# Streaming attention pairs of batch 0 with joint scores, and a new order of the kernel's head

## The chip, the cores and the metric

The kernel runs on one core of a Trainium2 chip. The metric is the device time of one launch in microseconds (us); lower is better. The kernel before took 227.66 us in the median of three runs (226.22 to 230.84).

## What is computed

The input is an attention layer (4 batches, 8 heads, 768 positions, 64 channels a head) and a two-layer MLP. Three heads (0, 2 and 6) are retrieval heads with a full causal mask. The other five are streaming heads: a position sees the 4 first positions and the 64 latest ones.

```python
scores = (1 / sqrt(64)) * q @ k.T
mask   = causal                       if retrieval head
         causal & (sink | in_window)  otherwise          # sink: key < 4, window: 64
a      = softmax(where(mask, scores, -1e9))
x      = (a @ v)                      # heads side by side: [3072, 512]
h      = x @ w_in                     # [512, 2048]
g      = maximum(h, 0) + alpha * minimum(h, 0)
out    = g @ w_out                    # [2048, 512]
```

## The kernel before

**Units of work.** A segment n is a pair of heads of one batch: batch n // 4, heads PAIRS[n % 4] of (2, 6), (1, 5), (0, 4), (3, 7). So in each batch pair 0 is two retrieval heads, pairs 1 and 3 are two streaming heads, and pair 2 has one of each. Batch 0 (n below 4) is handled in a way of its own: its masks are added on PE as extra matmuls (the identity times a mask of -30000) rather than multiplied in afterwards on DVE.

**Steps of a segment,** with the letters that the order uses:

- Lq, Lk, Lv: loads of q, k and v as fp32. SP issues them, but for the first half of k of pair 0 (`load_k`, L230), which ACT issues. Lq0 is split by head into Lq0.0 and Lq0.1.
- Cq, Ck, Cv: casts to bf16. The strings CQ, CK and CV (L303 to L305) say for each n which engine does it: V is DVE, A is ACT, P is POOL. A cast of v in batch 0 is followed by a small copy of the sink rows for each streaming head (`sinks`, L308), on POOL by default.
- Tq, Tk: transposes on PE (`to_array`); tq, tk: the copies of them out of PSUM (`put_q`, `put_k`). For streaming heads `put_k` lays the keys out in 7 slots of 128 (sinks and window) with three copies (L400 to L402). Each head has a key array of its own, of 128 rows, of which its own 64 hold keys and the others zeros (items kz0 to kz3 clear them).
- S, s: scores on PE (`S_retr`, `S_stream`) and their exponentials on ACT (`E_retr`, `E_stream`). A streaming head of batch 0 has 7 score matmuls, over all 128 rows, and 7 mask matmuls, in thirds of 384 columns; its exponentials are one of two thirds and one of one.
- A, a: attention times v on PE (`AV`), and the division by the sum on DVE.
- X, x: transposes of the result into xT (on PE and DVE in batch 0, by DMA later).
- P, p, g: the first projection (`P1`), the negative part on ACT (`relu`) and the combination on DVE (`prelu`). P0.f.part is the projection of the first 512 positions for one block f of 128 of the 2048 columns; for f below 6 it is cut into the parts that need pairs 0 and 1, pair 2, and pair 3. t = 0 and t = 1 are batch 0.
- O, o: the second projection and its way out. L, l: the last piece of it.
- wi0 to wi7 and wo0 to wo3: loads of w_in and w_out, issued by POOL. wi0 and wi1 hold the two halves of the contraction for f 0 to 3, wi2 and wi3 for f 4 to 7, wi4 and wi5 for 8 to 11, wi6 and wi7 for 12 to 15.
- warm0 to warm8: groups of matmuls on a zero tile (L698), which compute nothing.
- id, nms, nmr, zero, one, vz, qz, sz, so, kfz, nz: constants and clears.

**Order.** ORDER (L14) is a list of all these items, written by a planner, and `kernel` issues them in that order (L817). An engine runs its own instructions in the order in which they were issued; waits across engines follow from the data. A DMA that POOL issues stands in POOL's own queue between its casts and clears. SP has the loads alone in the head.

**PSUM.** Eight banks. Scores of batch 0 take a pair of banks out of (0, 1) and (2, 3).

The head of ORDER, up to the projections P1.8, P0.8 and P0.10, covers the loads, casts and attention of batch 0 and the first blocks of its projection. In this head POOL's queue has, as far as the prediction needs it: Ck3.1, Ck3.0, wi1, wi0, Cq3, Cv1 and its two sink copies, two clears, Cv2 and its sink copy, a clear, wi6, wi7, wi5, wi4, Cv3.0.

Of the kernel before, what the change touches and what calls it, by code (L numbers as in the profile page):

```python
# [14 lines left out]
vz2 id busy warm4 warm0 warm5 vz0 qz0 Lq0.0 sz2 so2 Lq0.1 zero vz3 nms Lk1 Lq1 sz1  # L15
Cq0.1 nmr Ck1.1 kz1 La Lk0 Ck1.0 kz0 Cq1 Cq0.0 Tq0.0 Ck0.0 Tk0.0 tk0.0 Lk2 Ck2.0 Lv0 warm2
tq0.0 S0.0.0 s0.0.0 qz S0.0.1 Tk1 warm3 warm6 vo kz2 Ck0.1 vz1 Ck2.1 Tq1 s0.0.1 tq1 Tq0.1 tk1.1
S0.0.2 s0.0.2 Cv0 tk1.0 m4.0.2 warm7 tq0.1 Lq2 S1.1.0 Tk0.1 tk0.1 S1.0.0 ro0 s1.1.0 Tk2 tk2.1 idf Cq2
s1.0.0 S0.1.0 s0.1.0 A0.0 S0.1.1 s0.1.1 S0.1.2 Tq2 warm8 s0.1.2 tq2 S1.1.1 s1.1.1 A0.1 kz3 sz0 Lk3 Ck3.1
Lv1 S1.0.1 m4.1.2 a0.0 s1.0.1 Al Ck3.0 Lq3 tk2.0 Tk3 S2.0.1 s2.0.1 a0.1 tk3.1 al X0 x0 S2.0.2  # L20
Lv2 Lv3 so1 so0 Lq5 wi1 s2.0.2 Lk4 m8.0.2 wi0 Cq3 Tq3 S2.0.0 s2.0.0 tk3.0 Cv1 tq3 A1.0
a1.0 Lk5 kfz2 A1.1 a1.1 kfz0 S2.1.0 S2.1.1 Cv2 s2.1.1 kfz3 wi6 A2.0 a2.0 wi7 S3.1.0 s2.1.0 s3.1.0
wi5 wi4 S3.0.0 A2.1 Cv3.0 s3.0.0 X1 S3.1.1 s3.1.1 S3.0.1 a2.1 X2 x1 x2 m8.1.2 near2 Ck4.0 P0.0.0
wi2 s3.0.1 A3.0 Cv3.1 P0.3.0 a3.0 P0.2.0 P0.2.1 A3.1 Ck4.1 Lk7 Lk6 P0.1.0 P0.1.1 P0.0.1 Tk4 tk4.0 Cq5
m14.0.2 a3.1 X3 nz1 tk4.1 x3 Tq5 P0.3.1 tq5 P1.2 p1.2 P1.0 p1.0 g1.0 P0.1.2 wi3 P0.13 Lq4
one p0.1 g0.1 P0.2.2 Lq6 Lv7 p0.2 P0.0.2 P1.14 p1.14 g1.2 g1.14 Ck5.0 Ck5.1 nr Tk5 tk5.1 P0.3.2
tk5.0 g0.2 p0.0 g0.0 p0.3 g0.3 P0.12 p0.12 g0.12 p0.13 g0.13 P0.14 nz0 kfz1 P1.8 P0.8 wo0 p0.8
g0.8 P0.10 S5.1.1 s5.1.1 P0.15 p0.15 wo1 wo2 wo3 ns p1.8 g0.15 g1.8 P0.11 p0.11 p0.14 g0.14 p0.10
S5.0.0 Lv5 P0.7 g0.10 P0.6 Ck6.1 P0.4.0 Lq7 P0.4.1 Lk8 Ck6.0 s5.0.0 p0.7 S5.0.2 s5.0.2 Cq4 Tq4 tq4
g0.11 P0.4.2 P0.9 Ck7.1 Ck7.0 S5.1.0 p0.9 g0.9 P1.4 s5.1.0 p1.4 Lv6 S4.0.1 Cq6 m12.1.2 P0.5.0 s4.0.1 P0.5.1  # L30
P0.5.2 P1.12 m5.0.0 g1.4 S4.0.3 g0.7 p0.4 p0.5 m5.1.0 g0.4 g0.5 Cv5 P1.10 S5.0.1 p1.10 s5.0.1 near0 p0.6
g0.6 O0.1.0 Tq6 s4.0.3 m4.0.3 Tk6 tk6.1 tk6.0 O0.2.0 P1.6 p1.6 m5.0.1 Tk7 tk7.1 Lv4 S4.0.2 O0.2.1 g1.6
ro1 tq6 p1.12 s4.0.2 tk7.0 O0.1.1 O0.2.2 O0.1.2 g1.10 S4.0.4 S4.0.0 S5.1.2 g1.12 S4.0.5 S4.1.4 S4.1.0 s4.0.4 s4.0.0
m5.1.1 m4.0.4 s4.1.0 m4.1.0 m5.0.2 O0.1.3 s5.1.2 O0.3.0 O0.2.3 Cq7 m5.1.2 Ck8 Tq7 near1 A5.1 o0.1 S6.1.0 s4.1.4
s6.1.0 O0.3.1 a5.1 s4.0.5 O0.3.2 O0.3.3 m4.0.1 m4.0.5 Cv4 tq7 S7.0.0 S6.0.5 S7.1.1 S4.1.1 Lk9 Lk10 Lq9 o0.2
o0.3 S4.1.3 S7.0.1 A5.0 s4.1.1 s7.0.0 m4.0.0 a5.0 X5 A4.0 s7.0.1 Lk11 s7.1.1 a4.0 s4.1.3 O1.1.0 m4.1.3 Cv7
s6.0.5 m7.0.0 m7.1.1 Lq8 S7.1.0 S6.0.4 S7.0.2 S4.1.5 S6.0.1 S7.1.2 S6.1.1 O1.1.1 Cv6 s7.1.0 O1.0.0 s4.1.5 m7.0.1 s6.1.1
m4.1.5 m6.1.1 s7.1.2 m6.1.0 s7.0.2 m7.0.2 S6.0.2 S4.1.2 S6.1.2 S6.0.0 s6.0.4 s4.1.2 s6.0.1 s6.1.2 O1.0.1 m6.0.5 m7.1.0 m4.1.1
# [24 lines left out]
m12.0.5 A12.0 s14.0.1 s12.1.4 O5.1.3 Dk15.1 s14.1.1 Dk15.0 s14.0.0 a12.0 m14.0.1 Dq15 o5.1 O4.2.1 S13.1.2 S12.1.2 S14.1.2 S14.0.4
m13.1.0 m14.0.0 m13.0.1 S14.0.5 S13.0.0 O4.2.2 O4.2.3 s13.1.2 m13.1.2 m13.1.1 s13.0.0 s14.0.4 s14.0.5 m13.0.2 S12.1.0 m12.1.5 s14.1.2 S12.1.3
S15.0.0 S14.0.3 m13.0.0 A13.1 o4.2 s12.1.0 s12.1.2 A13.0 s15.0.0 O5.0.0 s12.1.3 s14.0.3 m14.0.4 Cv15 a13.1 O5.0.1 a13.0 S15.0.1
S15.0.2 m12.1.0 S15.1.0 S15.1.2 S15.1.1 S14.0.2 O4.1.0 s15.0.2 s15.1.0 m12.1.4 s14.0.2 s15.1.1 m14.1.1 m14.0.5 m14.1.2 m12.1.3 m14.1.0 A12.1
m14.0.3 A14.1 A14.0 s15.1.2 m15.0.0 m15.0.2 m15.1.0 s15.0.1 m15.1.1 O4.1.1 X13 m15.1.2 m15.0.1 a14.0 a14.1 A15.0 A15.1 a12.1
O4.0.0 X14 O4.0.1 O4.0.2 O4.0.3 X12 o4.0 a15.0 O4.1.2 a15.1 O4.1.3 X15 o4.1 O5.0.2 O5.0.3 o5.0 P6.11 p6.11
P6.2 P6.15 P6.10 p6.10 P7.4 P6.0 P6.1 g6.11 g6.10 p6.1 P6.6 P7.8 p6.15 g6.15 g6.1 p6.0 g6.0 P6.5
p7.4 p6.5 p6.6 g7.4 g6.6 g6.5 P6.3 P6.12 P7.2 p6.3 p6.12 g6.12 p6.2 g6.2 P6.4 p7.8 P7.6 P6.14  # L70
g6.3 g7.8 p7.6 p6.4 g7.6 g6.4 P7.10 P6.7 P6.8 p6.8 p6.7 P7.0 P6.9 P6.13 g6.7 p7.2 g7.2 g6.8
p7.10 g7.10 p6.9 P7.14 O6.3.0 P7.12 p6.13 g6.13 p7.12 O6.0.0 O6.0.1 O6.1.0 p7.0 g7.0 g6.9 O6.3.1 O7.0.0 O6.3.2
O6.1.1 p7.14 p6.14 g6.14 g7.12 O6.3.3 o6.3 O6.0.2 O6.1.2 O6.1.3 o6.1 O6.0.3 o6.0 O6.2.0 O6.2.1 O6.2.2 O7.0.1 O7.0.2
O6.2.3 o6.2 m12.0.2 g7.14 L2 l2 O7.0.3 o7.0 L0 L1 l1 warm1 l0
""".split()


@with_exitstack
def kernel(
    ctx: ExitStack,  # L80
    tc: tile.TileContext,
    q: bass.AP,
    k: bass.AP,
    v: bass.AP,
    is_retrieval: bass.AP,
# [117 lines left out]
    def heads(n):  # L203
        return PAIRS[n % 4]
# [5 lines left out]
    def load_q(n, eng=nc.sync):  # L210
# [647 lines left out]
```

## Time and profile before

| what | value |
|---|---|
| median of three runs | 227.66 us |
| lowest and highest run | 226.22 and 230.84 us |
| span of the profiled execution | 225.1 us |
| PE busy | 219.3 us, 97% of the span |
| ACT, DVE, POOL busy | 139.5, 148.0, 45.3 us |
| mean granted clock of PE | 0.998 |
| HBM read and written | 27.71 and 6.29 MB |

The span is the time from the first to the last instruction of one profiled execution; a run's time is longer by what lies around it. The profiled execution has no time of its own beside its span, so 225.1 us stands against the runs' median of 227.66 us.

How to read the profile's lines: PE is the matmul engine, PEld its weight loader, DVE, ACT and POOL the vector, scalar and general engines, SP the engine that issues loads. L607 is line 607 of the kernel. In the list of waits, "A <- B: 1.2, 1, 1.2" is the total idle time of A that B ended, the number of times and the longest. In the table by stretches, each engine has its busy time and its instructions, and the last three columns are PE's granted clock, the mean busy share of the 16 DMA engines and GB/s. In the timeline and the chain a line starts with its start and its duration in us; on PE the duration has the pipeline's delay in it, so the distance between starts tells the pace.

### The profile page before, as it was taken

The numbers are of one execution on the slowest core, as the hardware profiler recorded it, in microseconds if no ns is written. First come the engines' busy times: TensorE is split into PE (matmuls) and PEld (weight loads), VectorE is DVE, ScalarE is ACT, GpSimd is POOL, SyncE is SP. The second block draws the span as 40 slices with busy tenths as digits, with TensorE's granted clock in tenths as the row PEclk, the third lists the DMA queues.
The fourth block names the chain that finished last, engine by engine and source line by source line (L and its number), as shares of the span: only waits on it lengthen the run. The fifth ranks groups of instructions, "written<-read, shape, count | busy, mean of one in ns | idle before, by whom it ended". The sixth has DMA issues, their size and how long they took to land.

```text
span 225.1 us, 5178 instructions
## 1 busy us (share of the span) xinstructions
PE 219.3 (97%) x1958; PEld 136.0 (60%) x1986; DVE 148.0 (66%) x395; ACT 139.5 (62%) x286; POOL 45.3 (20%) x91
## 2 busy tenths in 40 slices
PE   7999999999999999999999999999999999999995
PEld 7989876575555557554556455556557455664454
DVE  5799638995659618898799129977589226866000
ACT  3788668999888027577993137787594237563311
POOL 5678849500230001000401001000110110000000
PEclk9999999999999999999999999999999999999999
DMA  6999999999999999999989898995721620000213
GB/s 199 310 242 197 276 215 282 210 196 224 198 233 225 146 239 177 208 197 180 242 191 188 208 250 179 177 179 112 129 95 39 152 96 0 0 1 3 89 64 128
DMA packets 96185, 37.58 MB, mean 167 GB/s; under 512 B 83208, under 2 KB 94368, under 8 KB 96160
## 3 DMA queue, kind: packets, MB, share of 16 engines
q1 hardware_dynamic: 89904, 27.92, 65.5%
q0 software_dynamic: 5792, 8.93, 18.0%
q10 hardware_dynamic: 464, 0.40, 0.6%
q8 instruction: 15, 0.25, 0.5%
q14 instruction: 10, 0.08, 0.1%
HBM read 27.71 MB, written 6.29 MB: 151 GB/s over the span
## 4 chain that ended last, share of the span: by engine, by line
PE 84%; SPq 9%; DMA 2%; issue 2%; ACT 1%; DVE 0%; POOL 0%; DVEq 0%; POOLq 0%; ACTq 0%
PE P L627 31%; PE P L607 31%; PE P L562 7%; SPq L249 6%; PE P L438 3%; PE P L421 3%; PE P L698 3%; DMA vf<-in_v_dram 2%; SPq L253 2%; PE P L646 2%; SPq L246 2%; PE P L371 1%; PE P L508 1%; PE P L587 1%; PE P L431 1%
## 5 line engine op out<-in xcount | busy, mean ns | idle before, releaser
L619 DVE SCALAR_TENSOR_TENSOR g<-neg,oma,P 128x256 bf16<-128x256 f32 (+1 forms) x128 | 71.0, 609 | 41.4 <-ACT neg L612 40.8
L607 PE MATMUL P<-xT,w_in_b 128*128 128x256 bf16 (+1 forms) x501 | 85.7, 325 | 0.6
L627 PE MATMUL P<-w_out_b,g 128*128 128x512 bf16 x351 | 83.0, 379 | 1.0 <-issue 0.2
L612 ACT ACTIVATE neg<-P 128x512 f32<-128x512 f32 x96 | 54.2, 600 | 26.3 <-PE P L607 17.4
L607 PEld LDWEIGHTS <-w_in_b 128*128 128x128 bf16 x512 | 49.5, 98 | 32.3 <-DVE g L619 0.2
L627 PEld LDWEIGHTS <-g 128*128 128x128 bf16 x368 | 33.9, 98 | 37.4 <-issue 0.9
L477 ACT ACTIVATE eR<-P 128x448 bf16<-128x448 f32 (+3 forms) x63 | 35.9, 614 | 5.4 <-PE P L438 2.5
L633 ACT COPY ot<-P 128x512 f32<-128x512 f32 x23 | 13.8, 600 | 36.9 <-PE P L627 31.4
L637 POOL DMA_DIRECT2D out_dram<-ot x18 | 10.3, 574 | 108.5 <-ACT ot L633 108.3
L524 ACT ACTIVATE eS<-P 128x352 bf16<-128x352 f32 x45 | 20.4, 479 | 3.8 <-PE P L438 3.4
L573 DVE TENSOR_TENSOR xn<-P,rcp 128x448 bf16<-128x448 f32 (+1 forms) x32 | 19.0, 595 | 1.1
L535 DVE TENSOR_TENSOR eS<-eS,ms_near 128x352 bf16<-128x352 bf16 x45 | 14.6, 335 | 0.9 <-ACT eS L524 0.6
L486 DVE TENSOR_TENSOR eR<-eR,mr_near 128x128 bf16<-128x128 bf16 x54 | 10.2, 218 | 3.9 <-ACT eR L477 3.7
L421 PE MATMUL P<-qT,kT 128*128 128x192 bf16 (+14 forms) x68 | 11.2, 251 | 0.2 <-DVE kT L394 0.2
L572 DVE RECIPROCAL rcp<-P 128x7 f32<-128x7 f32 (+1 forms) x32 | 6.3, 196 | 7.6 <-PE P L562 7.0
L562 PEld LDWEIGHTS <-eS 128*128 128x128 bf16 x266 | 9.7, 97 | 2.3 <-issue 0.6
L562 PE MATMUL P<-vb,eS 128*128 128x65 bf16 x266 | 10.8, 193 | 0.0
L438 PEld LDWEIGHTS <-kT 64*128 64x128 bf16 x167 | 6.7, 94 | 6.1 <-issue 5.5
L438 PE MATMUL P<-qT,kT 64*128 64x176 bf16 (+7 forms) x167 | 10.3, 250 | 0.0
L562 PE MATMUL P<-vb,eR 128*128 128x65 bf16 x258 | 9.9, 193 | 0.1
L562 PEld LDWEIGHTS <-eR 128*128 128x128 bf16 x258 | 9.1, 97 | 1.4 <-issue 0.2
L655 DVE COPY ot<-P 128x128 f32<-128x128 f32 x1 | 0.3, 292 | 14.3 <-PE P L646 14.3
(96 smaller groups left out, 175.2 us busy)
## 6 DMA issues: line engine op xcount, KB each, us to landing
out_dram<-ot POOLq DMA_DIRECT2D x18, 256.0 KB, 4.1
kf<-in_k_dram SPq DMA_DIRECT2D x21, 192.0 KB
qf<-in_q_dram SPq DMA_DIRECT2D x18, 192.0 KB
vf<-in_v_dram SPq DMA_DIRECT2D x14, 196.0 KB
qf<-in_q_dram SPq DMA_DIRECT2D x7, 384.0 KB
vf<-in_v_dram SPq DMA_DIRECT2D x12, 192.0 KB
w_in_b<-in_moe_w_in_dram POOLq DMA_DIRECT2D x8, 256.0 KB, 9.5
w_out_b<-in_moe_w_out_dram POOLq DMA_DIRECT2D x4, 512.0 KB, 13.8
```

Source lines behind the costliest of these rows:

```text
L421: nc.tensor.matmul(to, keys, queries, start=True, stop=stop)
L438: nc.tensor.matmul(to, keys[own], queries[own], start=True, stop=True)
L477: nc.scalar.activation(ebuf[n, hh][:, lo:hi].rearrange("p (x c) -> p x c", x=len(parts)), P[:, got[0]:got[0] + len(parts), 0:(hi - lo) // ...
L524: nc.scalar.activation(slots, sc[:, 0:352].rearrange("p (s c) -> p s c", c=176), AF.Exp, scale=scale)
L535: nc.vector.tensor_tensor(slots, slots, ms_near[:, 0:2, :] if m == 0 else ms_near[:, 1:3, :], op=ALU.mult)
L562: nc.tensor.matmul(pav[:, i, :], e[:, o:o + 128], vv[:, j, hh, 0:D + 1], start=(m == 0), stop=(m == len(terms) - 1))
L573: nc.vector.tensor_tensor(xn[n][:, 0:nt, D * hh:D * hh + D], pav[:, :, 0:D], rcp.to_broadcast([128, nt, D]), op=ALU.mult)
L607: nc.tensor.matmul(psg[:, w * i:w * (i + 1)], w_in_b[:, c, 128 * fb:128 * (fb + 1)], xT[:, c, o:o + w], start=(x == 0), stop=(x == 3))
L612: nc.scalar.activation(neg[t, f], bank(held["P", t, f][0]), AF.Relu, scale=-1.0)
L619: nc.vector.scalar_tensor_tensor(g_buf[t % 2][:, fb, 0:w], neg[t, f][:, c], oma[:, fb:fb + 1], bank(got[0])[:, c], op0=ALU.mult, op1=ALU.add)
L627: nc.tensor.matmul(bank(held["O", t, s][0]), g_buf[t % 2][:, f, 128 * s:128 * (s + 1)], w_out_b[:, f, :], start=(f == 0), stop=(f == 15))
L633: nc.scalar.copy(ot, bank(got[0]))
```

## The change

In words:

- **Joint scores** for the streaming pairs of batch 0 (n = 1 and 3, JOINT). `put_k` writes both heads' keys into one array, the first head's into rows 0 to 63 and the second's into rows 64 to 127, with three copies of 128 rows for the pair. `S_joint` takes two banks, one a head; each bank gets one mask matmul of all the third's columns, and then the scores, alternately from the two row halves of the array. `E_joint` makes the exponentials of both heads for one third in one instruction. So a pair has three items J and three items j instead of four S and four s. The mask tile nms is 384 columns wide for this.
- **Loads of pair 0:** Lk0.0 and Lk0.1 are separate items, both on SP. SP's queue begins q0.0, k0.0, q1, k1, k2, k0.1, q0.1, v0, q2, where it began q0.0, q0.1, k1, q1, k0.1, k2, v0, q2 (k0.0 was on ACT). From q2 on it is as before.
- **Filler matmuls:** the counts of warm0 to warm8 go from 32, 3, 14, 4, 4, 4, 4, 4, 4 to 32, 3, 0, 3, 1, 2, 4, 0, 1.
- **Engines of casts and copies:** the cast of q of pair 3 goes from POOL to ACT; of k of pair 3 from POOL to DVE; of k of segment 4 from POOL to ACT, of segment 5 to DVE; of v of pair 1 from POOL to DVE (its sink copies stay on POOL); the second half of k of pair 0 from POOL to DVE. The copy of q of pair 2 goes from ACT to DVE, that of the second q half of pair 0 from DVE to ACT. The clears kz1 and kz2 go to POOL and kz3 to DVE.
- **Order of the head:** a new list up to P1.8; from there both lists are the same. In POOL's queue, wi1 now stands behind the cast of q of pair 2, and then come the two sink copies of pair 1, kz1, Cv2 and its sink copy, wi0, wi6, wi7, Cv3.0 and its sink copy, a clear, wi5, the cast of q of segment 5, a clear, wi4, wi2, a clear, wi3, wo0. On PE, X2 stands behind P0.0.0 and P0.1.0, where it stood before P0.0.0.

The core of the diff:

```diff
-            (nc.scalar if n == hh == 0 else nc.sync).dma_start(
+            if n == 0 and hh != of:
+                continue
+            nc.sync.dma_start(
...
-    nms = const.tile([128, 192], bf16, name="nms")
-    nms6 = const.tile([128, 44], bf16, name="nms6")
+    nms = const.tile([128, 384], bf16, name="nms")
+    nms6 = nms[:, 340:384]
...
+        nc.gpsimd.tensor_copy(nms[:, 192:340], nms[:, 0:148])
...
-    CQ = "VPPPPPAAVVVVVVVV"
-    CK = "APPPPPVVVVVVVVVV"
-    CV = "PPPPPPVVVVVVVVVV"
+    CQ0, CK0 = "VP", "AV"
+    TQ0, TQ = "AA", " AVAAAAA"
+    KZ = "VPPV"
+    WARM = (32, 3, 0, 3, 1, 2, 4, 0, 1)
+    CQ = "VPPAPPAAVVVVVVVV"
+    CK = "APPVAVVVVVVVVVVV"
+    CV = "PVPPPPVVVVVVVVVV"
...
+    JOINT = (1, 3)
...
-        rows = slice(64 * hh, 64 * hh + 64)
+        rows = slice(0, 128) if n in JOINT else slice(64 * hh, 64 * hh + 64)
...
+    def S_joint(n, m):
+        held["J", n, m] = got = take(*SC2)
+        pieces = []
+        o = 0
+        for j, w in THIRD[m]:
+            pieces.append((j, o, w))
+            o += w
+        mask = nms if m == 2 else nms[:, 0:192].unsqueeze(1).to_broadcast([128, 2, 192])
+        for b in got:
+            nc.tensor.matmul(bank(b)[:, 0:o], ident, mask, start=True, stop=False)
+        for j, o, w in pieces:
+            for x, b in enumerate(got):
+                own = slice(D * x, D * x + D)
+                nc.tensor.matmul(bank(b)[:, o:o + w], kTs[n][0][own, 128 * j:128 * (j + 1)],
+                                 qT[n][own, 124 * j:124 * j + w], start=False, stop=j == pieces[-1][0])
+
+    def E_joint(n, m):
+        got = held.pop(("J", n, m))
+        to = eS_all[:, 0:2, 2 * m * SLOT:2 * (m + 1) * SLOT].rearrange("p n (s c) -> p n s c", c=SLOT)[:, :, :, 0:192]
+        nc.scalar.activation(to, P[:, got[0]:got[0] + 2, 0:384].rearrange("p n (s c) -> p n s c", c=192), AF.Exp, scale=scale)
+        give(got)
```

The new ORDER around the loads of w_in (the old one had `so0 Lq5 wi1 s2.0.2 Lk4 m8.0.2 wi0 Cq3`):

```
... A0.1 Ck3.0 j1.0 S2.0.0 s2.0.0 warm5 Tk3 Cv1 S2.1.1 s2.1.1 a0.1 Lv3 A1.0 a1.0 S2.0.2 m8.1.2 Cq3
warm7 kz1 m4.1.2 s2.0.2 Lq5 A1.1 Lk4 Cv2 Lk5 Lk7 S2.0.1 wi0 s2.0.1 Lk6 a1.1 tk3.0 X0 wi6 ...
s2.1.0 wi7 Lq6 J3.1 Cv3.0 nz1 j3.1 wi5 A2.0 x0 a2.0 J3.2 A2.1 a2.1 J3.0 kz3 j3.2 P0.0.0 Cq5 j3.0 ...
```

More of the change, by code (lines that the diff above doesn't have):

```diff
@@ L14 @@
 ORDER = """
[L15 to L26, printed above, removed]
@@ L71 @@
[L71 to L74, printed above, removed]
+sz1 so1 busy warm2 zero kj Lq0.0 Cq0.0 vz2 vz1 Lk0.0 qz0 id m14.0.2 Ck0.0 warm0 Lq1 kz0 Tq0.0 Tk0.0 sz0 so0 Lk1 tk0.0
@@ L401, in put_k @@
         small(slots[:, 6, a:a + S // T - z, :], src[:, z:S // T, :])
-        small(slots[:, :, 0:a, :], src[:, 0:a, :].unsqueeze(1).to_broadcast([64, 7, a, T]))
+        small(slots[:, :, 0:a, :], src[:, 0:a, :].unsqueeze(1).to_broadcast([rows.stop - rows.start, 7, a, T]))
     ebuf, n_e = {}, [0, 0]
@@ L719 @@
         fill(f"vz{i}", vf[i][:, 6, :, :], 0.0)
-    for i in (0, 1, 2):
-        fill(f"kz{i}", kT_all[:, i].bitcast(fp32), 0.0)
-    fill("kz3", kT_all[:, 3].bitcast(fp32), 0.0, nc.gpsimd)
+    for i in range(NK):
+        fill(f"kz{i}", kT_all[:, i].bitcast(fp32), 0.0, {"P": nc.gpsimd, "V": nc.vector}[KZ[i]])
+    fill("kj", kT_all[:, 1:4:2, 0, 792:896].bitcast(fp32), 0.0)
     fill("qz", qT_all[:, :, S:S + 32].bitcast(fp32), 0.0)
@@ L734 @@
     item("nmr", causal_mask)
-    for i, n in enumerate((32, 3, 14, 4, 4, 4, 4, 4, 4)):
+    for i, n in enumerate(WARM):
         item(f"warm{i}", warm, n)
@@ L750 @@
         fill(f"nz{i}", NATK[i].bitcast(fp32), 0.0, nc.gpsimd)
+        item(f"Lk0.{i}", load_k, 0, i)
         item(f"Lq0.{i}", nc.sync.dma_start, part_of(qf[0], i), dram(q, PAIRS[0][i] * S * D, [[6 * D, 128], [1, 6 * D]]))
@@ L760 @@
             item(f"Cq{n}", cast_q, n)
-        item(f"Lk{n}", load_k, n)
+        if n:
+            item(f"Lk{n}", load_k, n)
         item(f"Lv{n}", load_v, n)
@@ L773 @@
                 item(f"Tq{n}", lambda n=n, two=two: to_array(("q", n), natq[n], two))
-                item(f"tq{n}", put_q, ("q", n), n, slice(0, 128), "A")
+                item(f"tq{n}", put_q, ("q", n), n, slice(0, 128), TQ[n])
                 item(f"Tk{n}", lambda n=n, two=two: to_array(("k", n), natk[n], two))
-                for hh in range(2):
-                    item(f"tk{n}.{hh}", put_k, ("k", n), n, hh, True)
+                for hh in range(1 if n in JOINT else 2):
+                    item(f"tk{n}.{hh}", put_k, ("k", n), n, hh, n not in JOINT)
         else:
@@ L782 @@
                 item(f"Dk{n}.{hh}", dma_k, n, hh)
+        for m in range(3 if n in JOINT else 0):
+            item(f"J{n}.{m}", S_joint, n, m)
+            item(f"j{n}.{m}", E_joint, n, m)
         for hh, h in enumerate(heads(n)):
```

112 lines of the change are left out of this document (62 added, 50 removed).

## The prediction

> **What bounds the kernel now.** I read the page's busy times first, then who waited for whom on PE, then busy times by stretch, then the chain of waits.
>
> ```profile
> PE 219.3 (97%) x1958; PEld 136.0 (60%) x1986; DVE 148.0 (66%) x395; ACT 139.5 (62%) x286; POOL 45.3 (20%) x91
> ```
> ```profile
> PE P L698 <- DVE busy L295: 1.2, 1, 1.2
> PE P L421 <- DVE kT L394: 0.2, 1, 0.2
> ```
> ```profile
> 15.00:26.08 11.08, 11.03 (x206) 10.34 (x204) 9.23 (x27) 9.55 (x15) 9.27 (x19) 1.00 1.12 251
> 26.08:39.34 13.26, 13.15 (x117) 8.73 (x119) 8.43 (x21) 9.80 (x21) 9.97 (x18) 1.00 1.18 243
> 39.34:65.13 25.79, 25.55 (x205) 15.23 (x207) 18.14 (x51) 23.73 (x52) 5.46 (x15) 1.00 1.17 212
> ```
>
> PE is busy for 97% of the span and waits for others 1.4 us in all, of which 1.2 are the start. PE takes its instructions in the order written, so the end is the sum of what stands in its queue: an us of work or of waiting put in anywhere appears at the end. The second limit is in the stretches, columns share of the DMA engines (last but one) and GB/s: from 15 to 65 us the DMA engines are full as well (1.12 to 1.18). [...] The chain shows the one place where both meet:
>
> ```profile
> 58.72 4.33 DMA vf<-in_v_dram
> 64.15 0.94 POOL vb L356
> 65.13 0.79 PE P L562 x21
> ```
>
> V of pair 4 lands, POOL casts it until 65.09, and PE starts A4.0 at 65.13. PE's own rows around that place, in order of time:
>
> ```profile
> 64.48 0.57 PE L562 MATMUL P<-vb,eS 128*128 128x65 bf16 x13
> 65.13 0.79 PE L562 MATMUL P<-vb,eR 128*128 128x65 bf16 x21
> 65.77 1.02 PE L627 MATMUL P<-w_out_b,g 128*128 128x512 bf16 x3
> ```
>
> The 21 of A4.0 take 0.64 us from their start to the next row's, 0.03 us each. The 13 before them need 0.39 us by that measure and are through at 64.87, so PE already stands still for 0.25 us there. Time won before 65 us is lost again at A4.0, unless V of pair 4 also comes sooner. Time lost before 65 us is lost, less 0.25 us.
>
> **The change, part by part.** ORDER differs only before the projection P1.8; from there it is the old one, item for item. I split the head at the first projection, P0.0.0, PE's first matmul of L607:
>
> ```profile
> 26.08 0.38 PE L607 MATMUL P<-xT,w_in_b 128*128 128x512 bf16 x1
> ```
>
> *Filler matmuls.* Of the 70 filler matmuls (L698) before P0.0.0, 43 stay.
>
> ```profile
> 1.21 4.45 PE P L698 x40
> 8.78 0.45 PE P L698 x8
> ```
>
> The opening block goes from 40 to 32: 8 x 0.111 us (4.45/40) = 0.89. Nineteen later ones go: 19 x 0.056 (0.45/8) = 1.06. Together 1.95 us of PE work goes. What was hidden behind the fillers (the first Q and K copies) becomes waiting in their place.
>
> *Streaming pairs 1 and 3.* Today each head of such a pair has 14 matmuls, scores and masks one by one.
>
> ```profile
> 22.63 0.24 PE L421 MATMUL P<-qT,kT 128*128 128x192 bf16 x1
> 23.95 0.55 PE L562 MATMUL P<-vb,eS 128*128 128x65 bf16 x13
> 25.11 0.24 PE L421 MATMUL P<-qT,kT 128*128 128x192 bf16 x1
> 25.46 0.56 PE L587 MATMUL P<-ident,xn 128*128 128x128 bf16 x7
> ```
>
> Sixteen of 192 columns start in 1.32 us (0.0825 each); six for the last third take 0.35. A head is 8 x 0.0825 + 0.35 = 1.01, four heads 4.04 us. In the new form a third has two masks of 384 columns (0.165 each) and its scores in two 64-row halves; if the halves run beside each other, 0.165 for both heads: 0.495 x 6 = 2.97, a gain of 1.07. The later pairs show the 64-row form already, and its price:
>
> ```profile
> PEld L438 <- issue: 5.5, 14, 0.4
> ```
>
> Each of 14 bursts keeps the weight loader idle for 0.39 us with nothing to wait for but the change of form. Six thirds pay this zero to six times: 0 to 2.3 us. So the pairs are worth between -1.07 and +1.3 us; I take the middle, +0.1. The three copies fewer per pair on DVE and one exponential fewer on ACT lie beside PE work. All of this stands ahead of P0.0.0, so PE reaches P0.0.0 between 26.08 - 1.95 - 1.07 = 23.1 and 26.08 - 1.95 + 1.3 = 25.4; I take 24.2.
>
> *X2 changes sides.* The transposes of pair 2 stood before P0.0.0 and stand behind it now; nothing else crosses.
>
> ```profile
> 24.50 0.39 PE P L587 x7
> ```
>
> So P0.0.0 must start by 26.08 - 0.39 = 25.69 us for the rest to be on time.
>
> *Loads on SP.* The same bytes; K of pair 0 goes to SP's queue in two parts, the first sooner, the second and the second Q part behind K of pairs 1 and 2. From Q of pair 2 on, the order is the old one.
>
> ```profile
> kf<-in_k_dram SPq DMA_DIRECT2D x21, 192.0 KB
> ```
>
> A half's 192 KB take 0.8 us at the 251 GB/s of the stretch up to 26.08. With full DMA engines I leave V of pair 2 where it lands, and allow one such half either way.
>
> *W_in on POOL: the step that decides.* P0.0.0 waits for the pieces 0 and 1 of w_in. Today POOL issues them together; the pieces 6, 7, 5, 4 come behind the V cast of pair 2:
>
> ```profile
> 15.51 1.42 POOL L703 DMA_DIRECT2D w_in_b<-in_moe_w_in_dram  x2
> 20.33 0.93 POOL L356 CAST vb<-vf 128x896 bf16<-128x896 f32 x1 [0.20 <-DMA vf<-in_v_dram]
> 21.33 0.34 POOL L313 COPY vb<-vb 4x192 f32<-4x192 f32 x1
> 21.77 2.45 POOL L703 DMA_DIRECT2D w_in_b<-in_moe_w_in_dram  x4
> ```
>
> In the changed program's POOL queue only piece 1 stands before; then come the sink copies of pair 1 (behind DVE's cast now), a clear of kT, the V cast of pair 2, its sink copy, and only then pieces 0, 6 and 7. The cast cannot start before V of pair 2 has landed (20.33, with 0.20 of waiting in its row). So piece 0 is issued at 20.33 + 0.93 + 0.07 + 0.34 + 0.03 = 21.7, not at 16.3. The times from issue to landing, one issue each (those at 15.51, 16.29, 21.77 us):
>
> ```profile
> DMA to landing us min/median/max: 6.4/6.4/6.4
> DMA to landing us min/median/max: 7.4/7.4/7.4
> DMA to landing us min/median/max: 7.9/7.9/7.9
> ```
>
> Piece 0 takes the very slot of the third of these. It lands between 21.7 + 6.4 = 28.1 and 21.7 + 7.9 = 29.6; I take 28.7, as three are issued together, between the pair and the four. PE, there at 24.2, stands for 4.5 us. P0.0.0 starts 28.7 - 25.69 = 3.0 us late; less the 0.25 at A4.0, 2.8 us. The pieces 6 and 7 land some 2 and 4 us after piece 0 (the pair's 7.4 after 16.29 against 6.4 after 15.51 is 1.8 apart) and are first used behind Tk5, whose row today is this, 8.4 us after P0.0.0, with 1.7 us of projections (P0.13, P1.14) before it that now come later: no second wait.
>
> ```profile
> 34.46 0.50 PE L371 MATMUL P<-ident,natm 128*128 128x128 bf16 x6
> ```
>
> W_out is issued no later than now, and V of pair 4 is no longer late for PE. Queued behind P0.0.0 is the whole of PE; ACT and DVE run dry and catch up.
>
> *The clock.* The opening block ran at 0.111 us for 128 columns, the later eight at 0.056: PE starts at half its clock. At the end of the run it falls back:
>
> ```profile
> 219.00:222.30 3.30, 3.30 (x38) 2.75 (x36) 0.02 (x1) 0.99 (x3) 0.00 (x0) 1.00 0.50 179
> 222.30:224.40 2.10, 0.05 (x1) 0.00 (x0) 0.27 (x1) 0.00 (x0) 0.00 (x0) 1.00 0.30 98
> 224.45:225.10 0.65, 0.00 (x0) 0.00 (x0) 0.00 (x0) 0.00 (x0) 0.00 (x0) 0.50 0.00 0
> ```
>
> 2.1 us of idleness sufficed for a granted clock of 0.50; 4.5 us is twice that, so I expect the drop. The way back took the 4.45 us block and a little more. [...]
>
> *Casts moved between engines* (K of pairs 3, 4, 5, Q of 2 and 3, V of 1): nothing, since they are done while PE waits at P0.0.0; were that wait gone, ACT with 9.55 of 11.08 us busy would be the next cover to fail.
>
> **Sum.** 3.0 - 0.25 + 1.6 = 4.35. The profiled execution has a span of 225.1 us, so 229.5 after; the runs' median is 227.66 (226.22 to 230.84), 2.6 us above that span, and I take that distance as unchanged: 232.0 us, 1.9% above the median. Two per cent, about what a measurement of this kernel can tell from no change, is 232.2.
>
> **The rivals.**
> (a) Piece 0 is late and the clock holds: 227.66 + 2.8 = 230.4. For it: the clock's row is one case at the end. Against: the wait is twice as long.
> (b) Not slower: piece 0 lands by 25.69. It needs 4.0 us from issue to landing, or V of pair 2 some 3 us earlier. Then every saving ends at A4.0, where V of pair 4 is awaited: 0 to 0.25 us, about 227.4. For it: POOL's output stores land in a median of 4.1 us (row below). Against: those have a quieter time; no w_in row is under 6.4. [...]
> (c) The savings reach the end: V of pair 4 comes 3 us sooner too: 227.66 - 1.95 - 1.07 = 224.6. Against: the loads ahead of it are the same bytes through full engines.
> [...]
>
> ```profile
> out_dram<-ot POOLq DMA_DIRECT2D x18, 256.0 KB, 4.1
> ```
>
> **How the numbers follow.** The forecast (late, with a drop) 0.53, (a) 0.17, (b) 0.20, (c) 0.04, (d) 0.06. Predicted: 232.0, the forecast's own range being 230.0 to 233.8. To leave out no more than 2 in 10 the range takes in (b) and ends within (d): 227.2 to 233.8. Over 2% slower is (d) and the half of the forecast that lies above 232.2: 0.33. Over 2% faster needs more than (c): 0.02. Within 2%: 0.65.
>
> **What would show it.** Right: PE idle of 3 to 5 us ahead of the first projection, ended by w_in's landing; the second w_in issue on POOL behind the V cast of pair 2, at 21 to 22 us; matmuls of 512 columns at twice their time for some us after it, and a granted clock of 0.5 there; from A4.0 on the old chain, shifted; no wait for V of pair 4. Wrong: the first projection before 25.7 us, or piece 0 landing within 5 us of its issue; or PE ahead of 65 us at A4.0 without a wait, which would mean that loads had come sooner than I allow.

## The result, and the profile after

The changed kernel takes 233.12 us in the median of four runs (232.04 to 234.04); the kernel before, beside it, 227.33 us (226.22 to 230.84). The ratio is 1.0271, with a 95% interval of 1.0223 to 1.0319: slower by more than two per cent. The forecast was 232.0 us and a range of 227.2 to 233.8. The profiled execution is the slowest of the four, 234.04 us with a span of 232.3, so it stands 7.2 us above the span of before and shows a little more loss than the median. (The ratios, here and below, leave out runs more than 1.5% above the fastest of their kernel; medians and ranges hold every run.)

The page's busy times of after, and then who waited for whom on PE:

```profile
PE 221.6 (95%) x1943; PEld 132.7 (57%) x1943; DVE 147.6 (64%) x395; ACT 140.7 (61%) x287; POOL 40.9 (18%) x84
```
```profile
PE P L635 <- DMA w_in_b<-in_moe_w_in_dram: 5.1, 1, 5.1
PE P L726 <- DVE zero L295: 1.5, 1, 1.5
PE P L375 <- POOL g L326: 1.1, 1, 1.1
```

There is one new large wait, and it is for w_in (the first projection is now L635). POOL's timeline shows where that load stood, and the row of its DMA alone how long it took from issue to landing:

```profile
13.04 0.77 POOL L731 DMA_DIRECT2D w_in_b<-in_moe_w_in_dram  x1
20.68 0.93 POOL L360 CAST vb<-vf 128x896 bf16<-128x896 f32 x1 [1.64 <-DMA vf<-in_v_dram]
21.68 0.34 POOL L317 COPY vb<-vb 4x192 f32<-4x192 f32 x1
21.97 1.85 POOL L731 DMA_DIRECT2D w_in_b<-in_moe_w_in_dram  x3
```
```profile
DMA to landing us min/median/max: 8.1/8.1/8.1
```

PE's timeline around the wait (start, duration, work), and its busy times by stretch, whose third column from the end is the granted clock:

```profile
24.68 0.34 PE L531 MATMUL P<-qT,kT 64*128 64x192 bf16 x4
30.17 1.87 PE L635 MATMUL P<-xT,w_in_b 128*128 128x512 bf16 x4 [5.15 <-DMA w_in_b<-in_moe_w_in_dram]
...
33.31 1.47 PE L635 MATMUL P<-xT,w_in_b 128*128 128x512 bf16 x3
34.57 0.92 PE L590 MATMUL P<-vb,eS 128*128 128x65 bf16 x13
...
36.60 0.38 PE L635 MATMUL P<-xT,w_in_b 128*128 128x512 bf16 x1
36.81 0.55 PE L615 MATMUL P<-ident,xn 128*128 128x128 bf16 x7
...
71.91 0.57 PE L590 MATMUL P<-vb,eS 128*128 128x65 bf16 x13
72.32 0.80 PE L590 MATMUL P<-vb,eR 128*128 128x65 bf16 x21
```
```profile
24.70:30.00 5.30, 0.32 (x5) 0.10 (x4) 1.43 (x2) 2.62 (x6) 5.30 (x10) 0.92 1.07 165
30.00:36.00 6.00, 5.83 (x42) 3.53 (x43) 1.82 (x5) 0.00 (x0) 0.54 (x1) 0.50 1.20 220
36.00:65.00 29.00, 29.00 (x221) 18.33 (x219) 22.16 (x53) 25.77 (x56) 7.31 (x18) 1.00 1.13 227
```

PE is through with what stands ahead of the first projection at about 25.0 us, stands until 30.17, and then works at half speed until 36.0: by the distance between starts, a matmul of 512 columns takes 0.42 us at 33.31 ((34.57 - 33.31) / 3) and 0.21 us at 36.60. The last two rows of the timeline answer to the pair shown of before (64.48 and 65.13 us). The first is 7.43 us late, the second 7.19 us: the 0.24 us by which PE waited for V of pair 4 are all that is made good. A shift of 7.43 us stands on the instructions from 46.77 us on (39.34 in the kernel before), and one of 7.19 us on those from 72.32 us to the end.

So the profiled 7.2 us are these: the first projection starts 30.17 - 26.08 = 4.09 us later; between it and 46.77 us another 7.43 - 4.09 = 3.34 us are lost, 0.39 us of it in the work that stands behind it now (X2) and the rest in the main in the clock; 0.24 us are recovered.

### The profile page after: what moved, and what is told of

Its sections match the earlier page's. It is cut to its first block, busy times and chain, and to the rows that moved or that the text cites. A ratio compares the mean times of both kernels' runs of the same rounds, so it can differ in the third digit from the quotient of the medians.

```text
span 232.3 us, 5120 instructions
## 1 busy us (share of the span) xinstructions
PE 221.6 (95%) x1943; PEld 132.7 (57%) x1943; DVE 147.6 (64%) x395; ACT 140.7 (61%) x287; POOL 40.9 (18%) x84
## 4 chain that ended last, share of the span: by engine, by line
PE 86%; DMA 8%; SPq 3%; POOL 1%; issue 0%; DVE 0%; DVEq 0%; POOLq 0%
PE P L635 37%; PE P L655 35%; PE P L590 6%; PE P L444 4%; DMA w_in_b<-in_moe_w_in_dram 3%; DMA vf<-in_v_dram 3%; DMA kf<-in_k_dram 2%; PE P L674 2%; PE P L437 1%; SPq L251 1%; PE P L375 1%; SPq L212 1%; SPq L228 1%; PE P L615 0%; POOL vb L360 0%
## 5 line engine op out<-in xcount | busy, mean ns | idle before, releaser
L635 PE MATMUL P<-xT,w_in_b 128*128 128x512 bf16 (+1 forms) x512 | 88.6, 330 | 5.1 <-DMA w_in_b<-in_moe_w_in_dram 5.1
L655 PE MATMUL P<-w_out_b,g 128*128 128x512 bf16 x368 | 85.1, 379 | 0.0
L635 PEld LDWEIGHTS <-w_in_b 128*128 128x128 bf16 x512 | 49.8, 98 | 38.2 <-issue 6.4
L492 DVE TENSOR_TENSOR eR<-eR,mr_near 128x128 bf16<-128x128 bf16 x54 | 10.7, 230 | 3.8 <-ACT eR L483 3.7
L590 PEld LDWEIGHTS <-eS 128*128 128x128 bf16 x266 | 10.4, 101 | 2.5 <-issue 1.1
L590 PE MATMUL P<-vb,eS 128*128 128x65 bf16 x266 | 11.8, 198 | 0.0
L400 ACT COPY kT<-P 64x768 bf16<-64x768 bf16 x3 | 2.4, 793 | 9.7 <-PE P L375 9.7
```

The source lines that it names most:

```text
L492: nc.vector.tensor_tensor(ej, ej, mr_near, op=ALU.mult)
L590: nc.tensor.matmul(pav[:, i, :], e[:, o:o + 128], vv[:, j, hh, 0:D + 1], start=(m == 0), stop=(m == len(terms) - 1))
L635: nc.tensor.matmul(psg[:, w * i:w * (i + 1)], w_in_b[:, c, 128 * fb:128 * (fb + 1)], xT[:, c, o:o + w], start=(x == 0), stop=(x == 3))
L655: nc.tensor.matmul(bank(held["O", t, s][0]), g_buf[t % 2][:, f, 128 * s:128 * (s + 1)], w_out_b[:, f, :], start=(f == 0), stop=(f == 15))
```

## The experiments

The theory was the prediction's: piece 0 of w_in stands behind the cast of V of pair 2 in POOL's queue, lands late, and the wait also costs PE its clock. The rivals were that the new form of the scores, the fewer fillers or the moved casts cost the time, and that the place of the load in POOL's queue does not matter. Twelve kernels were run:

| kernel | median (range), us | ratio to before (95%) |
|---|---|---|
| e1_piece0_early | 228.23 (226.94 to 232.19) | 1.0037 (1.0007 to 1.0068) |
| e2_only_piece0_late | 232.05 (231.35 to 234.79) | 1.0257 (1.0201 to 1.0314) |
| e3_fillers_in_the_wait | 231.07 (230.84 to 232.87) | 1.0202 (1.0167 to 1.0237) |
| e4_early_and_v4_first | 228.06 (226.78 to 231.06) | 1.0027 (0.9992 to 1.0062) |
| e6_early_and_start_fillers | 228.33 (226.20 to 231.79) | 1.0021 (0.9985 to 1.0058) |
| e7_after_and_start_fillers | 233.96 (233.12 to 234.49) | 1.0299 (1.0241 to 1.0357) |
| e8_before_without_its_fillers | 227.55 (226.88 to 230.84) | 1.0038 (1.0007 to 1.0069) |
| e10_early_v4_start_fillers | 228.32 (227.03 to 232.50) | 1.0021 (0.9981 to 1.0062) |
| e11_early_two_waits_less | 228.86 (226.72 to 231.89) | 1.0048 (1.0012 to 1.0084) |
| e12_two_waits_less_v4_first | 228.19 (226.69 to 231.40) | 1.0030 (0.9997 to 1.0064) |
| e13_piece0_before_cast | 228.32 (226.41 to 231.08) | 1.0037 (1.0008 to 1.0066) |
| e14_piece0_between | 226.67 (226.20 to 227.30) | 0.9982 (0.9962 to 1.0002) |

The kernel before, run beside them, had medians of 227.04 to 227.46 us and single runs of up to 234.12 us. The diffs are of items in ORDER, unless they show code.

### One step alone, and one step undone

e2 takes the kernel before and moves piece 0 only:

```diff
-Lk4 m8.0.2 wi0 Cq3 Tq3
+Lk4 m8.0.2 Cq3 Tq3
...
-s2.1.1 kfz3 wi6
+s2.1.1 kfz3 wi0 wi6
```

> The kernel before with one step moved: the load of piece 0 of w_in is issued behind the cast of V of pair 2 and the copy of its sink row, directly ahead of piece 6, with everything else as it was. Theory: this alone makes the loss. The piece is issued at about 21.8 us and lands at about 29.5 to 30, the first projection starts 3.5 to 4 us later than 26.1, the matmuls after it run at half the clock for some us (1.5 to 2.2 us more), and 0.25 us are recovered in front of V of pair 4: 232.4 us, between 231.5 and 233.5. Rival (the load is ordered early enough wherever POOL issues it, and the loss came from the joint scores or the casts): 227.3 us, within 1 us of the kernel before.

Measured: 232.05 us, 1.0257. PE's waits, its timeline and its stretch:

```profile
PE P L607 <- DMA w_in_b<-in_moe_w_in_dram: 3.4, 1, 3.4
```
```profile
29.66 0.59 PE L607 MATMUL P<-xT,w_in_b 128*128 128x512 bf16 x2 [3.40 <-DMA w_in_b<-in_moe_w_in_dram]
```
```profile
30.00:36.00 6.00, 6.00 (x60) 3.79 (x58) 2.22 (x5) 0.99 (x2) 0.55 (x2) 0.72 1.18 237
```

The start is 29.66 - 26.08 = 3.58 us late, as expected, and the clock drops (0.72 over six us). One moved load makes nearly the whole loss, with the old scores, fillers and casts all in place. The rival that blames those falls.

e1 undoes the step in the changed kernel:

```diff
-wi1 Lv2
+wi1 wi0 Lv2
...
-S2.0.1 wi0 s2.0.1
+S2.0.1 s2.0.1
```

> The changed kernel with one step moved: the load of piece 0 of w_in is issued directly behind that of piece 1, at about 13 us, instead of at 22.0 us behind the cast of V and the copy of the sink row. Theory (the late piece 0 and the clock that it costs are the whole loss): the first projection starts at about 25 us without a wait, its 512-column matmuls take 0.216 us each from the start, and the head's saving of about 1 us is lost in front of the fourth pair's V at 65 us, as before the change; 227.0 us, between 226.4 and 227.8. Rival (the joint scores, the fewer fillers or the casts in another order cost the time, and the wait for piece 0 only hid it): 230 us or more although no wait for w_in is left. Rival (the saving of the head reaches the end): 226 us or less.

Measured: 228.23 us, 0.4 above the upper bound given. No wait for w_in is left, and 4.9 of the 5.8 us are back (233.12 - 228.23, of 233.12 - 227.33). But the kernel does not quite come out level with the kernel before, and its times reach 232.19 us. The rest of the study is about this last us.

### The price of the clock

e3 gives PE work in the wait:

```diff
+        for i in range(84 if t == f == cs[0] == 0 else 0):
+            nc.tensor.matmul(psg[:, 0:128], busy, busy, start=True, stop=True)
```

> The changed kernel with 84 more matmuls that compute nothing needed, 128 columns each, 0.056 us by the fillers' row, 4.7 us in all, written directly ahead of the first projection into the bank that it has taken, so that TensorE has work while it waits for piece 0 of w_in. Theory (the wait costs 4.5 us and the clock that drops in it about 2.2 us): the first projection still starts at about 30.2 us, its 512-column matmuls take 0.216 us from the start, granted clock 1.0 in 30 to 36 us; 230.9 us, between 230.3 and 231.6. Rival (the clock costs nothing at the end, since the time is made good in front of a later wait): as the changed kernel, 233.1 us.

Measured: 231.07 us, that is 2.05 us below the changed kernel in the medians. Its timeline and its stretch; three matmuls of 512 columns take 0.81 us, with the pipeline's delay, against 1.47 above, and the granted clock is 1.00 against 0.50:

```profile
31.77 1.02 PE L637 MATMUL P<-xT,w_in_b 128*128 128x512 bf16 x4 [1.58 <-DMA w_in_b<-in_moe_w_in_dram]
33.42 0.81 PE L637 MATMUL P<-xT,w_in_b 128*128 128x512 bf16 x3
```
```profile
30.00:36.00 6.00, 4.42 (x61) 3.00 (x59) 2.39 (x6) 0.00 (x0) 1.52 (x3) 1.00 1.20 221
```

The clock held, although this profiled execution (232.87 us, the slowest of its four) got its piece 0 later still. From the start of the first projection to the end of the span it is 231.2 - 31.77 = 199.4 us here and 232.3 - 30.17 = 202.1 us in the changed kernel: 2.7 us for the clock in the profiled pair, 2.05 in the medians, and 1.6 by the ratios (1.0271 - 1.0202, whose intervals overlap). The rival that the clock costs nothing falls; how much it costs is less sharp.

### The start of the clock: a theory that fell

In e1's profile the first projection started at 27.00 us, not at 25. PE's timeline says why:

```profile
7.65 0.82 PE L375 MATMUL P<-ident,g 128*128 128x128 bf16 x6 [1.11 <-POOL g L326]
8.26 0.58 PE L427 MATMUL P<-qT,kT 128*128 128x448 bf16 x1
...
11.79 0.83 PE L375 MATMUL P<-ident,g 128*128 128x128 bf16 x12
12.46 0.49 PE L527 MATMUL P<-nms,ident 128*128 128x384 bf16 x2
...
27.00 1.04 PE L635 MATMUL P<-xT,w_in_b 128*128 128x512 bf16 x4
```

Where the kernel before has 14 fillers, PE waits 1.11 us for the cast of pair 1's q, and in this execution it works at half speed until about 11 us: six matmuls of 128 columns take 8.26 - 7.65 = 0.61 us, 0.10 each, and twelve later ones 12.46 - 11.79 = 0.67 us, 0.056 each. In the profile of the changed kernel the same wait did not do that (six take 0.35 us, from 7.08 to 7.43). So I took the loss of the last us for a late clock. e6 fills the gap:

```diff
-    WARM = (32, 3, 0, 3, 1, 2, 4, 0, 1)
+    WARM = (32, 3, 0, 3, 1, 2, 4, 0, 1, 16)
...
-Cq1 Ck1.0 La Tq1
+Cq1 Ck1.0 La warm9 Tq1
```

> The kernel of e1_piece0_early with 16 more matmuls that compute nothing needed, 128 columns each, written directly ahead of the transposes of pair 1's queries, where TensorE idles 1.1 us at 6.5 us. In the profile of e1_piece0_early the matmuls ran at half speed until 11.2 us, in that of the changed kernel only until 5.4 us, and the first projection started 2.05 us later for it; its runs lay between 226.94 and 232.19 us. Theory (with that gap some executions get the full clock late, and that is the 1.2 us by which e1_piece0_early was above the kernel before): with the gap filled the clock is full by 6 to 8 us, the first projection starts at about 25.0 us, 226.9 us median, between 226.4 and 227.4, and the times scatter no more than those of the kernel before. Rival (the slower runs have another cause): 228.2 us, scattered as e1_piece0_early.

Measured: 228.33 us, scattered as e1. The fillers did their work (in its profile six matmuls of 128 columns take 0.35 us at 7.29 us, 0.058 each, and the first projection starts at 25.19 us), and the time did not follow. Its waits name two others:

```profile
PE P L375 <- POOL natq L326: 1.7, 1, 1.7
PE P L635 <- DVE xT L620: 1.1, 1, 1.1
```

The theory of the late start fell. Two controls do not bring it back. e7 has the same 16 fillers and piece 0 late:

> The changed kernel with the same 16 matmuls ahead of the transposes of pair 1's queries, piece 0 of w_in as late as the change has it. Theory: the first projection starts when piece 0 lands, at about 30.1 us, whether the clock was full early or not, so that the start of the clock is hidden here: 232.6 us, between 231.8 and 233.3. Rival (the gap at the start is a loss of its own on top of the wait): 231.2 us or less.

Measured: 233.96 us, 0.7 above its range: no gain. Why it is slower than expected is not shown by a run of its own; all four of its executions have a mean clock of 0.985, and the last section says what that stands for. e8 takes the 14 fillers out of the kernel before (the third of its counts becomes 0):

> The kernel before without the 14 matmuls that compute nothing needed at 6.6 us, ahead of its first scores; nothing else changed. Theory (a gap of some 0.7 us at 6.6 us leaves it to chance when the clock becomes full): a median 0.5 to 1.5 us above the kernel before, 228.0 us, between 227.5 and 228.6, in some executions half-speed matmuls until about 11 us. Rival (those matmuls are only padding): 227.0 us, or up to 0.3 us less.

Measured: 227.55 us, at the edge of the range; the ratio of 1.0038 is a small loss. Those fillers are worth 0.4% (0.1 to 0.7), and what they guard against is not the whole of the last us.

### The transfers behind piece 0

With piece 0 early, what does PE wait for? e4 and e10 exchange two loads of V, e10 with the fillers of e6:

```diff
-s5.1.0 p1.4 Lv6 S4.0.1
+s5.1.0 p1.4 Lv4 S4.0.1
...
-Tk7 tk7.1 Lv4 S4.0.2
+Tk7 tk7.1 Lv6 S4.0.2
```

> The kernel of e1_piece0_early with the loads of V of pairs 4 and 6 exchanged in their queue, so that V of pair 4 lands about 2 us sooner. Theory (the first attention product of pair 4, at 65 us, is where the saving of the head is lost): the saving passes it, 226.3 us, between 225.9 and 226.8, and some 0.7 us below e1_piece0_early. Rival (another load that comes just in time, the keys of pair 8 or the queries of pair 7 at 58 to 60 us, takes its place): the same as e1_piece0_early within 0.2 us. Rival (the loss of the change is not in piece 0 at all): 230 us or more in both.

> The kernel of e4_early_and_v4_first with the same 16 matmuls ahead of the transposes of pair 1's queries. e4_early_and_v4_first could not tell whether V of pair 4 limits, since its first projection came 2.7 us late in the profile. Theory (with an early clock TensorE comes to the first attention product of pair 4 sooner, and only the earlier V lets it through): 226.2 us, between 225.7 and 226.7, 0.5 us or more below e6_early_and_start_fillers. Rival (another transfer, the keys of pair 8 or V of pair 2, takes its place): the same as e6_early_and_start_fillers within 0.2 us.

Measured: 228.06 and 228.32 us, both as without the exchange. V of pair 4 was not what kept them back. PE's waits and POOL's timeline of e10:

```profile
PE P L590 <- POOL vb L360: 1.8, 1, 1.8
PE P L375 <- POOL natq L326: 0.6, 1, 0.6
```
```profile
14.09 1.41 POOL L731 DMA_DIRECT2D w_in_b<-in_moe_w_in_dram  x2
23.62 0.93 POOL L360 CAST vb<-vf 128x896 bf16<-128x896 f32 x1 [4.21 <-DMA vf<-in_v_dram]
```

The cast of V of pair 2 starts at 23.62 us, and not at 20.33 as in the kernel before or at 20.68 as in the changed one: V came late. Over all profiles of this order the cast starts at 20.2 to 21.7 us where piece 0 comes later (the changed kernel, e3, e7, e13, e14), and at 21.6 to 24.8 us where it stands right behind piece 1 (e1, e4, e6, e10, e11, e12). e11 and e12 take the two waits of e6 away, e12 with the exchange of e4:

```diff
-Cv2 Lk5 Lk7
+Cv2 Lk5 Lq4 Lk7
...
-Tq3 Lq4 X1
+Tq3 X1
...
-P0.2.0 Ck5.0 Ck4.1
+P0.2.0 Ck4.1
...
-P0.0.1 X3 x3 Tk4
+P0.0.1 X3 x3 Ck5.0 Tk4
```

> The kernel of e6_early_and_start_fillers with two more steps moved: the load of q of pair 4 ahead of that of the keys of pair 7 in SyncE's queue, and the cast of the first keys of pair 5 on VectorE behind the copy of the transposed X of pair 3. In the profile of e6_early_and_start_fillers TensorE waited 1.1 us at 31.6 us for that copy, which stood behind the cast, and 1.7 us at 46.7 us for the cast of q of pair 4, which landed at 45.8 us. Theory (with piece 0 early, the saving of the head is lost again at the transfers that come just in time, and these two are the next): both waits go, 226.6 us, between 226.0 and 227.3. Rival (the DMA engines are full until 65 us, so that a load moved up only pushes another one behind TensorE): 227.5 us or more, with a wait for another tile in their place.

> The kernel of e11_early_two_waits_less with the loads of V of pairs 4 and 6 exchanged, as in e4_early_and_v4_first. Theory (V of pair 4 at 65 us is the last transfer that comes just in time): 226.2 us, between 225.6 and 226.8, below the kernel before. Rival (another transfer takes its place): the same as e11_early_two_waits_less within 0.3 us, or above.

Measured: 228.86 and 228.19 us. Both theories fell, and the rivals were right in kind: the waits of 1.7 and 1.1 us are gone, and V of pair 2 took their place. (In number e12's rival missed: it allowed 0.3 us from e11, and e12 lies 0.67 below, with intervals that overlap.) PE's waits in e11, in an execution of 231.66 us; e10's above, in one of 229.16 us, has the same wait:

```profile
PE P L590 <- POOL vb L360: 3.1, 1, 3.1
```

So piece 0 has two bad places: behind V of pair 2 it is late itself (issued at 21.97 us in the changed kernel, landed 8.1 us later), and right behind piece 1, which this order issues at 13.3 to 14.4 us, V of pair 2 can be late (its cast at 24.84 us in e11). In the kernel before the two stood together as well, but at 15.51 and 16.29 us, and V was on time. e13 puts piece 0 ahead of the cast, which was to halve the delay:

```diff
-Lk4 Cv2 Lk5 Lk7 S2.0.1 wi0 s2.0.1
+Lk4 wi0 Cv2 Lk5 Lk7 S2.0.1 s2.0.1
```

> The changed kernel with the load of piece 0 of w_in issued directly ahead of the cast of V of pair 2 and not behind it, so at about 19.1 us and not at 22.0 us: half of the delay. Theory (the piece starts late because POOL waits with the cast for V, and lands about 8 us after its issue): it lands at about 27.1 us, TensorE waits about 2.2 us ahead of the first projection, and the clock drops for less time or not at all: 229.6 us, between 228.3 and 230.8. Rival (the place in POOL's queue does not matter, only the order among the bytes that the DMA engines are full with): the wait stays at 4 us or more and the time at 232.5 us or more.

Measured: 228.32 us, at the lower edge of the theory's range and far from the rival's 232.5. In its profile the issue came at 20.80 us, only 1.2 us sooner than in the changed kernel. The piece landed 6.7 us after its issue and not 8.1, and PE itself came to the first projection only at 26.8 us, so that it waited 1.0 us and not 2.2, and the clock held (a mean of 1.000 over the span). PE's waits and POOL's timeline:

```profile
PE P L635 <- DMA w_in_b<-in_moe_w_in_dram: 1.0, 1, 1.0
PE P L375 <- POOL natq L326: 0.6, 1, 0.6
```
```profile
20.80 0.63 POOL L731 DMA_DIRECT2D w_in_b<-in_moe_w_in_dram  x1
21.46 0.93 POOL L360 CAST vb<-vf 128x896 bf16<-128x896 f32 x1
```

e14 puts it between, with the fillers of e6 and the early q of pair 4 of e11:

```diff
-Tk3 Cv1 S2.1.1
+Tk3 Cv1 wi0 S2.1.1
```

> The changed kernel with three steps moved or added: the load of piece 0 of w_in directly behind the copies of V of pair 1 (issued at about 18.2 us, between the 13.9 us of e6_early_and_start_fillers and the 20.8 us of e13_piece0_before_cast), the load of q of pair 4 ahead of that of the keys of pair 7, and the 16 matmuls ahead of the transposes of pair 1's queries. In the profiles of e11 and e12, with piece 0 at 13.8 and 14.4 us, V of pair 2 came so late that its cast started at 24.8 and 24.3 us and TensorE waited 3.1 and 2.5 us; in e13, with it at 20.8 us, the cast started at 21.5 us and TensorE waited 1.0 us for piece 0. Theory (V of pair 2 and piece 0 share the engines, and a start between the two delays neither by more than 0.7 us): waits of at most 0.7 us ahead of the first projection, which starts at 25.5 to 26.2 us, 227.0 us, between 226.3 and 227.8, so at best the kernel before. Rival (the bytes that must land by 26 us are the limit, so that one of the two is always late): a wait of 1 to 3 us for V of pair 2 or for piece 0, 228.2 us or more.

Measured: 226.67 us, and all twelve runs lie within 226.20 to 227.30. POOL's timeline, PE's waits (all of them but the start's) and the start of the projection:

```profile
18.51 0.63 POOL L731 DMA_DIRECT2D w_in_b<-in_moe_w_in_dram  x1
20.24 0.93 POOL L360 CAST vb<-vf 128x896 bf16<-128x896 f32 x1 [0.24 <-DMA vf<-in_v_dram]
```
```profile
PE P L375 <- POOL g L326: 0.2, 1, 0.2
PE P L655 <- issue: 0.2, 1, 0.2
PE P L635 <- issue: 0.2, 1, 0.2
PE P L635 <- DVE xT L620: 0.2, 1, 0.2
```
```profile
25.48 0.81 PE L635 MATMUL P<-xT,w_in_b 128*128 128x512 bf16 x3 [0.16 <-issue]
```

Piece 0 is issued 3.7 us later than in e10 (18.51 against 14.09 + 0.7, the second of two issues), and V is on time; it is issued 3.5 us earlier than in the changed kernel, and is on time itself. The theory was right, the rival wrong. e11 shares the fillers and the early q with e14 and comes out at 1.0048 (1.0012 to 1.0084), clear of e14's interval. They differ in the place of piece 0, and in the cast of pair 5's first keys, which e14 leaves where the change has it. So with the fillers and the early q the last us is this place, but for that cast, which was not tried by itself; whether the place alone would do it in e1 was not run either.

With every large wait gone by these three steps, the changed kernel is level with the kernel before (0.9982, interval 0.9962 to 1.0002). Its first projection starts at 25.48 us, 0.60 us sooner; X2 and some small waits behind it take that back; the rest of the change is worth nothing that these runs can tell.

## Why the prediction was right or wrong

**The deciding step** was right in place and kind: piece 0 of w_in behind the cast of V, PE idle ahead of the first projection, the clock dropping. e2 shows it alone, e1 shows it undone. Its size was too small. The issue was put at 21.7 us and came at 21.97. The time from issue to landing was put at 6.4 to 7.9 us, and 7.0 was taken; it was 8.1, past the longest row that I had. The first projection was put at 28.7 us and started at 30.17. The late start was put at 3.0 us; with the limit of 25.69 us it was 4.48. In e2, the same slot took 3.58 us against 26.08. This term was mis-sized by 1.5 us in the profiled execution. I had taken a value between three rows, though the row for the very slot was the longest of them, 7.9.

**The clock** was put at 1.6 us. That was the author's estimate, and no run shows the ground for it; in its place the runs showed 6.0 us at a granted clock of 0.50 in the changed kernel, and a cost of 2.7 us in the profiled pair, 2.05 in the medians of e3 and 1.6 by the ratios: the term was right in size or too small. The late start, and with it perhaps the clock, is why the result is 2.7% and not the 1.9% of the forecast, and why the larger chance, on "within 2%", went to the wrong class. The loss, 7.2 us in the profiled execution and 5.8 us in the medians, is above the forecast's 4.35 us in both.

**PE's arrival** at the first projection was put at 24.2 us within 23.1 to 25.4, and was about 25.0. The prediction said in words that what the fillers had hidden becomes waiting, and gave that no number: most of it is the 1.11 us for the cast of pair 1's q.

**The joint scores** were put at +0.1 us, the middle of -1.07 and +1.3. PE's timeline of the changed kernel has one third of a pair in these rows; the next work starts at 11.10 us:

```profile
10.41 0.49 PE L527 MATMUL P<-nms,ident 128*128 128x384 bf16 x2
10.83 0.34 PE L531 MATMUL P<-qT,kT 64*128 64x192 bf16 x6
11.10 0.34 PE L726 MATMUL P<-busy 128*128 128x128 bf16 x3
```

A third takes 11.10 - 10.41 = 0.69 us, where masks and scores at their pace would take 0.495; six take 4.14 us, against 4.04 for the old form. The six matmuls of the two halves take 11.10 - 10.83 = 0.27 us, less than the 0.33 that they would need one after the other, so the halves do run beside each other at least in part; what a third takes beyond 0.495 us, about 0.2, I put down to the change of form, which no run shows alone. The term came out at +0.1, as put; but +0.1 was the middle of a wide range, so that the number agrees is luck. This is read from the trace; the joint form was not undone by itself.

**V of pair 4** was right to the digit: 0.25 us predicted, 0.24 recovered. But the prediction took it for the only place where gains before 65 us are lost. With piece 0 early there are several: V of pair 2 at 24 us, the copy of X3 at 31, q of pair 4 at 46. Rival (b), piece 0 on time in its late slot, would have needed 4.0 us to the landing and got 8.1.

**Casts moved between engines** at nothing: right under the wait. One of them, the keys of pair 5 on VectorE ahead of the copy of X3, did become a wait of 1.1 us in e6, once the cover was gone; the prediction had named ACT as the next to fail. In e14, with that cast in its place, the wait is 0.2 us.

**Rivals (a) and (c):** the clock did not hold, and no kernel of the study brought a clear saving to the end (e14's interval reaches 1.0002).

## What to carry to other kernels

When a load is issued by an engine that also computes, read what the instruction ahead of it in that engine's queue waits for before moving the load behind it: here piece 0 stood behind the V cast, which waited 1.64 us for V and started at 20.68 us, and was issued at 21.97 us. With transfer engines as full as here (a mean busy share of 1.07 to 1.20 from 24.70 to 65.00 us in the changed kernel), the load had a window, not a best early time: issued at 21.97 us it made its own user wait 5.15 us; issued right behind the issue at 14.09 us (e10) it stood ahead of a V whose cast came at 23.62 us; the place between the two, 18.51 us (e14), was found by looking at both landings. Price a wait on PE with the half-speed stretch that may follow it (after 5.15 us of waiting the granted clock was 0.50 for 6.0 us, after 1.8 us in e10 it stayed at 1.00), and price from the row of the very slot, not from the mean of its neighbours (7.9 us in the row, 7.0 taken, 8.1 measured).

## What the runs showed of the hardware

**The time from issue to landing changed with the slot.** Pieces of w_in of the same size took 5.9 us when issued alone at 18.5 us (e14), 6.7 at 20.8 (e13), 7.7 at 21.87 with four others behind it (e2) and 8.1 at 21.97 with two (after). Why the last is longer than the one before it stays open. The start of the V cast changed with the place of piece 0: 23.62 us with piece 0 issued right behind piece 1, at 14.09 us (e10), 20.24 with it at 18.51 (e14). How the one load delays the other is not shown.

**Which wait dropped the clock.** PE's wait of 1.8 us in e10 left the granted clock at 1.00 over the whole span. e12's waits and a stretch of it, in an execution of 230.22 us, show that less than the 3.4 us of e2 can be enough, as the 2.1 us at the end of the kernel before do (the rows at 219.00 to 225.10 us in the prediction):

```profile
PE P L590 <- POOL vb L360: 2.5, 1, 2.5
```
```profile
22.50:28.00 5.50, 3.02 (x42) 2.11 (x43) 1.18 (x3) 1.21 (x3) 3.62 (x7) 0.71 0.76 219
```

With a granted clock of 0.50 in the drop (29.20 to 35.90 us in the changed kernel), the half-speed time is what is missing from the mean clock, doubled: in e2 0.28 x 6.0 x 2 = 3.4 us, in the changed kernel 0.08 x 5.3 x 2 + 6.0 = 6.8 us, twice that.

**The price of a drop came in steps.** The mean clocks of all executions on record fall into three groups: 0.998 to 1.000, 0.992 to 0.993, and 0.985 (the opening block is not in them: from 1.21 to 5.66 us of the kernel before the granted clock reads 1.00, at 0.111 us a matmul of 128 columns). Over some 230 us these are none, one or two stretches at half speed of the length above (0.007 x 230 x 2 = 3.2 us, 0.015 x 230 x 2 = 6.9 us). One and the same kernel falls into different groups: the changed kernel had 0.985 three times (232.85 to 234.04 us) and 0.993 once (232.04 us), e2 had 0.993 three times (231.35 to 232.09 us) and 0.985 once (234.79 us). So the price of one wait differed from execution to execution. With piece 0 right behind piece 1, 17 of 71 executions lie in the two lower groups, of the kernel before 7 of 97, of e13 and e14 none of 22.
